# Idle TensorE products in float32r, fourteen of them moved behind the first unit's sums, and the first weight tile's shift done in one piece

## The chip, the cores and the metric

The kernel runs on one core of a Trainium2 chip. A core has TensorE (matrix products; the profile shows its weight loads apart, as PEld), VectorE (DVE), ScalarE (ACT), GpSimd (POOL) and SyncE (SP, which issues the transfers), and 16 DMA engines. The metric is device microseconds of one execution, and the number to compare is the median over runs.

## What is computed

Windowed attention for 4 batches of 576 tokens and 8 heads, then a gated layer, then a soft mixture of 8 experts with 4 slots each. Cut to its core:

```python
attn = softmax(mask(q @ k.T / 8)) @ v        # heads 0-3: window 32; heads 4-7: window 128, every 4th
x = attn as (2304, 512)
x = (sigmoid(x @ w_gate) * (x @ w_val)) @ w_out          # d_ff 1536
logits = x @ phi                                         # 32 slots
h = relu(softmax(logits, axis=tokens).T @ x @ w1) @ w2   # per expert
out = softmax(logits, axis=slots) @ h
```

The three weights of the gated layer come as float64 and are turned into float32 on the chip.

## The kernel before

**Tiling.** Tokens go in five blocks n: four of 512 and a last one of 256. Attention of a block is four units, each a pair of heads. A unit's steps are `scores` (64 small products into two PSUM banks after two mask products, L150 and L164), `soft_max`, `soft_exp`, `soft_sum`, `soft_norm`, `turn_unit` (four transposes on TensorE, L213, and a copy to `pt_ring` on ACT, L214), `sums` (products with the values, L240) and `finish_unit` (the result of each half split into a high part by ACT, L268, and a low part by DVE, L269). The trace shows a float32 product as two weight loads and two products, so the 32 products of `sums` stand there as 64 and 64.

**The gated layer.** For each of 12 column tiles f, 24 products 128x512 in float32r (L488): high and low parts of weights and of tokens. Its weights go through `convert_top` (ACT, L374), `convert_low` (DVE, L381), `convert_shift` (DVE, L378) and `convert_sum` (POOL, L385), and then `split_half` (ACT L445, DVE or POOL L446) into `whl`.

**The start of the program.** `first_block` (L890 to L977) writes out by hand, in program order for each engine, the attention of block 0, the conversion of weight tiles 0 and 1 and the first column tile's products. The order of TensorE there: idle products; scores of units 0 to 2 with idle products between; the transposes of unit 0; idle products; scores of unit 3; the transposes of unit 1; the sums of unit 0; the transposes of unit 2; the sums of unit 1; the first six products of the gated layer; the transposes of unit 3; the sums of unit 2; six products; the sums of unit 3 and 16 tiny ones (`pad_stream`); the last twelve products. The idle products (`keep_warm`, L108) multiply a block of zeros and their result is never read. They keep TensorE occupied between real work. After `first_block`, attention of later blocks is spread between the products of the gated layer, and everything on an engine waits its turn in that engine's queue.

**Names.** `pm` holds the zeros before. `fw` is the tile that is being converted and `st` the raw weights. `x_hi` and `x_lo` are the split tokens, `sm` a unit's softmax weights, `HALVES` and `WHOLE` the two halves or all of a tile's 1024 columns. `WARM` counts the idle products at the very start.

Of the kernel before, what the change touches and what calls it, by code (L numbers as in the profile page):

```python
# [8 lines left out]
F32R = mybir.dt.float32r  # L9
U32 = mybir.dt.uint32  # L10
I32 = mybir.dt.int32
BF16 = mybir.dt.bfloat16
# [5 lines left out]
P = 128  # L18
# [5 lines left out]
HIP = 200  # L24
LA = 2
WO_AT = (12, 13, 14, 15, 16, 17)
WARM = 3
PAD = 8
GA = 0
NRM = True  # L30
ND = 4
# [21 lines left out]
def tile_kernel(  # L53
# [25 lines left out]
    def b8(tag, shape, dt, name):  # L79
        return big.tile(shape, dt, tag=tag, name=name, bufs=BUFS[tag])  # L80
# [16 lines left out]
    pt_ring = b8("bd", [P, 4, 4, 4, 32], F32, "pt_ring")  # L97

    pm = cpool.tile([P, 2, 512], F32, name="pm")
    zero = pm[:, 0].bitcast(BF16)  # L100
    nc.vector.memset(zero, 0.0)
    idle = ps_l1.tile([P, 512], F32, tag="l1", name="idle")

    busy = {}
# [2 lines left out]

    def keep_warm(count):  # L108
        for _ in range(count):
            kept(nc.tensor.matmul(idle, lhsT=zero[:, 0:P], rhs=zero[:, 512:1024], start=True, stop=True))  # L110

    keep_warm(WARM)

# [75 lines left out]
    def soft_exp(u):  # L189
        kp(nc.scalar.activation(u["s"], u["s"], AF.Exp, scale=0.125))  # L190
# [185 lines left out]
    def convert_shift(fw, c):  # L376
        top = fw[:, 0, c].bitcast(U32)
        return kp(nc.vector.tensor_scalar(top, top, 3, None, ALU.logical_shift_left))  # L378

    def convert_low(z, fw, c):  # L380
        kp(nc.vector.tensor_scalar(fw[:, 1, c].bitcast(I32), staged[z][:, c, 0], 2.0**-29, None, ALU.mult))  # L381

    def convert_sum(fw, c):
        top, low = (fw[:, r, c].bitcast(I32) for r in range(2))
        kp(nc.gpsimd.tensor_tensor(low, top, low, ALU.add))  # L385
# [62 lines left out]
    def new_w():  # L448
        return b8("w", [P, 2, 2, ND, P], F32R, "whl")
# [435 lines left out]
    def sums(u, beside=None):  # L885
        if beside is None:
            beside = {"bank": [ps_a.tile([P, 512], F32, tag="a", name=f"x_ps{y}") for y in range(2)]}
        weighted(u, range(2), beside)

    def first_block():  # L890
        u = [{"id": (0, hp), "z": z} for z, hp in enumerate(HP_ORDER)]
        start_unit(u[0], "qk")
        ld(nc.sync.dma_start(msk, masks.bitcast(BF16)))
        start_unit(u[1], "qk")
        start_unit(u[2], "gb")
        ld(nc.sync.dma_start(cst, consts))
        stage(0)
        start_unit(u[3], "gb")
        for z in range(4):
            start_values(u, z)  # L900
        fw = [None, None]
        fw[0] = convert_begin(0)
        scores(u[0], range(4))
        soft_max(u[0])
        soft_exp(u[0])
        keep_warm(1)
        scores(u[1], range(4))
        soft_max(u[1])
        soft_exp(u[1])
        keep_warm(2)  # L910
        soft_sum(u[0])
        soft_norm(u[0], nc.gpsimd)
        scores(u[2], range(4))
        soft_max(u[2])
        soft_exp(u[2])
        soft_sum(u[1])
        soft_norm(u[1], nc.gpsimd)
        keep_warm(4)
        convert_top(0, fw[0], HALVES[0])
        turn_unit(u[0])  # L920
        convert_top(0, fw[0], HALVES[1])
        soft_sum(u[2])
        convert_low(0, fw[0], HALVES[0])
        convert_shift(fw[0], HALVES[0])
        convert_sum(fw[0], HALVES[0])
        soft_norm(u[2], nc.vector)
        convert_low(0, fw[0], HALVES[1])
        convert_shift(fw[0], HALVES[1])
        convert_sum(fw[0], HALVES[1])
        keep_warm(5)  # L930
        scores(u[3], range(4))
        turn_unit(u[1])
        soft_max(u[3])
        sums(u[0], u[2])
        finish_unit(u[0])
        soft_exp(u[3])
        whl = new_w()
        split_half(whl, fw[0][:, 1], 0, nc.vector)
        turn_unit(u[2])
        soft_sum(u[3])  # L940
        soft_norm(u[3], nc.vector)
        split_half(whl, fw[0][:, 1], 1, nc.vector)
        sums(u[1], u[3])
        finish_unit(u[1])
        convert_end(0, fw[0])
        first_qk()
        fw[1] = convert_begin(1)
        first_v()
        g = l1_tile(0, 0)
        pt = [ps_l1.tile([P, 512], F32, tag="l1", name="l1ps") for _ in range(2)]  # L950

        def chunk(dc):
            for a in range(2):
                l1_chunk(0, whl, a, pt[a], dc)

        chunk(HP_ORDER[0])
        turn_unit(u[3])
        for c in HALVES:
            convert_top(1, fw[1], c)
            convert_low(1, fw[1], c)  # L960
            convert_shift(fw[1], c)
            convert_sum(fw[1], c)
        sums(u[2])
        finish_unit(u[2])
        chunk(HP_ORDER[1])
        sums(u[3])
        pad_stream(u[3])
        finish_unit(u[3])
        chunk(HP_ORDER[2])
        whl1 = new_w()  # L970
        for h in range(2):
            split_half(whl1, fw[1][:, 1], h, nc.vector)
        convert_end(1, fw[1])
        chunk(HP_ORDER[3])
        for a in range(2):
            l1_gate(g, a, pt[a])
        return whl1  # L977
# [505 lines left out]
```

## Time and profile before

| | us |
|---|---|
| median of 3 runs | 484.9 (481.81, 484.9, 485.26) |
| the profiled execution, its own time | 486.59 |
| span of the profiled execution, first to last instruction | 484.8 |

| engine | busy us | share of the span |
|---|---|---|
| TensorE products | 466.3 | 96% |
| TensorE weight loads | 359.3 | 74% |
| DVE | 302.9 | 62% |
| ACT | 211.0 | 44% |
| POOL | 157.1 | 32% |

TensorE is the busy engine, and its busy share alone says little on how fast it goes: its clock has two levels, 1.2 and 2.4 GHz, and the profile gives the granted level for any stretch (1.00 is 2.4 GHz, 0.50 is 1.2 GHz). Over the whole span the mean is 0.983. A release named "issue" in the profile means that an engine waited for nothing that the profile records.

### The profile page before, as it was taken

How to read it: one execution, taken by the hardware profiler on the slowest of the kernel's cores; microseconds unless marked ns; L12 is line 12 of the kernel's file. 1: busy time of each engine (PE TensorE's matmuls, PEld its weight loads, DVE VectorE, ACT ScalarE, POOL GpSimd, SP SyncE). 2: the span in 40 equal slices, each digit the busy share in tenths (PEclk: the TensorE clock that was granted, in tenths of full speed). 3: DMA queues.
4: the chain of work that ended last, by engine and by line, in shares of the span. 5: the costliest groups of instructions: out<-in, count | busy, mean ns of one | idle time of the engine just before them, and what ended most of it. 6: DMA issues, size and time to landing. Idle time of an engine off the chain costs nothing.

```text
span 484.8 us, 12657 instructions
## 1 busy us (share of the span) xinstructions
PE 466.3 (96%) x5425; PEld 359.3 (74%) x5425; DVE 302.9 (62%) x595; ACT 211.0 (44%) x397; POOL 157.1 (32%) x134
## 2 busy tenths in 40 slices
PE   7799999999999999999999999999999999999993
PEld 3577788788778778787778888888888889842552
DVE  4868878847768766467876556656547765532623
ACT  2544555534546554454345554554525334300222
POOL 0325555504744654612033342324312124210100
PEclk9869999999999999999999999999999999999997
DMA  8978899786998783222220220201499886689976
GB/s 322 413 279 292 321 336 342 290 283 203 345 354 304 256 315 120 79 89 87 89 87 1 88 78 9 87 19 69 157 372 425 349 327 238 227 293 389 425 254 239
DMA packets 23720, 112.12 MB, mean 231 GB/s; under 512 B 2288, under 2 KB 7152, under 8 KB 14576
## 3 DMA queue, kind: packets, MB, share of 16 engines
q1 hardware_dynamic: 23664, 111.32, 61.7%
q8 instruction: 42, 0.69, 0.6%
q14 instruction: 14, 0.11, 0.1%
HBM read 97.16 MB, written 14.16 MB: 230 GB/s over the span
## 4 chain that ended last, share of the span: by engine, by line
PE 86%; DVE 4%; issue 3%; POOL 2%; ACT 2%; DMA 1%; SPq 0%; POOLq 0%; DVEq 0%; ACTq 0%
PE l1ps L488 30%; PE pa L612 13%; PE pe L612 7%; PE tp L745 4%; PE s_ps L240 3%; PE so_ps L1312 3%; PE pd L612 3%; PE h_ps L1250 3%; PE s_ps L164 3%; PE sp L770 2%; PE lt_ps L716 2%; PE tr L213 2%; POOL fw L385 1%; PE wt_ps L422 1%; PE op L1350 1%
## 5 line engine op out<-in xcount | busy, mean ns | idle before, releaser
L488 PE MATMUL l1ps<-x_hi,whl 128*128 128x512 f32 x384 | 131.4, 407 | 0.8 <-DVE whl L446 0.5
L488 PEld LDWEIGHTS l1ps<-x_hi,whl 128*128 128x128 f32 x384 | 73.1, 190 | 17.7 <-DVE whl L446 1.2
L488 PE MATMUL l1ps<-x_lo,whl 128*128 128x512 f32 x192 | 76.0, 396 | 0.0
L385 POOL TENSOR_TENSOR fw<-fw 128x512 int32<-128x512 int32 x36 | 47.4, 1332 | 51.2 <-DVE fw L378 31.4
L488 PEld LDWEIGHTS l1ps<-x_lo,whl 128*128 128x128 f32 x192 | 36.8, 191 | 6.5
L474 DVE SCALAR_TENSOR_TENSOR g<-g,l1ps 128x512 f32<-128x512 f32 (+1 forms) x36 | 21.4, 595 | 29.2 <-PE l1ps L488 29.2
L488 PE MATMUL l1ps<-x,whl 128*128 128x256 f32 x288 | 37.0, 285 | 0.0
L488 PEld LDWEIGHTS l1ps<-x,whl 128*128 128x128 f32 x288 | 35.4, 192 | 0.4 <-issue 0.2
L499 ACT ACTIVATE g<-l1ps 128x512 f32<-128x512 f32 (+1 forms) x36 | 19.0, 526 | 33.9 <-PE l1ps L488 33.9
L446 POOL TENSOR_TENSOR whl<-w,whl 128x512 fp32r<-128x512 f32 x12 | 15.9, 1327 | 51.2 <-ACT whl L445 39.7
L201 POOL TENSOR_TENSOR sm<-sm,su 128x512 f32<-128x512 f32 x14 | 18.1, 1292 | 27.1 <-DVE su L197 19.4
L745 PEld LDWEIGHTS tp<-cst,g 128*128 128x128 f32 x192 | 21.3, 140 | 5.4 <-issue 4.2
L745 PE MATMUL tp<-cst,g 128*128 128x128 f32 x192 | 25.0, 275 | 0.0
L446 DVE TENSOR_TENSOR whl<-fw,whl 128x512 fp32r<-128x512 f32 x24 | 20.9, 882 | 6.0 <-ACT whl L445 5.3
L750 ACT COPY gt<-tp 128x512 f32<-128x512 f32 x24 | 14.1, 586 | 24.2 <-PE tp L745 21.7
L446 POOL TENSOR_TENSOR whl<-wst,whl 128x512 fp32r<-128x512 f32 x12 | 15.9, 1321 | 25.9 <-ACT whl L445 20.9
L675 DVE TENSOR_TENSOR tm<-pe,tm 128x512 f32<-128x512 f32 x12 | 8.3, 692 | 24.7 <-PE pe L612 24.7
L445 ACT CAST whl<-fw 128x512 fp32r<-128x512 f32 x24 | 14.7, 620 | 19.7 <-POOL fw L385 13.0
L374 ACT ACTIVATE fw<-st 128x1024 f32<-128x1024 f32 (+1 forms) x20 | 21.0, 1057 | 4.5 <-DMA st<-wd 4.5
L240 PE MATMUL s_ps<-pt_ring,v 64*64 64x32 f32 (+1 forms) x992 | 18.3, 220 | 4.1 <-issue 4.0
L445 ACT CAST whl<-wst 128x512 fp32r<-128x512 f32 x24 | 14.3, 618 | 14.2 <-PE l1ps L488 8.6
L446 DVE TENSOR_TENSOR whl<-wst,whl 128x512 fp32r<-128x512 f32 x12 | 14.4, 1197 | 9.5 <-ACT whl L445 9.5
(483 smaller groups left out, 962.6 us busy)
## 6 DMA issues: line engine op xcount, KB each, us to landing
ew<-w SPq DMA_DIRECT2D x32, 1024.0 KB, 7.9
st<-wd SPq DMA_DIRECT2D x18, 1024.0 KB, 7.9
wst<-wg SPq DMA_DIRECT2D x12, 1024.0 KB, 5.9
v<-qkv SPq DMA_DIRECT2D x20, 512.0 KB, 7.2
wg<-fw SPq DMA_DIRECT2D x12, 512.0 KB, 5.6
w<-wg SPq DMA_DIRECT2D x6, 1024.0 KB, 6.4
qk<-qkv SPq DMA_DIRECT2D x10, 576.0 KB, 6.1
qk<-qkv SPq DMA_DIRECT2D x8, 528.0 KB, 6.1
```

What stands on the lines that cost most here:

```text
L164: nc.tensor.matmul(u["s_ps"][r][32 * i : 32 * i + 32, t, :], lhsT=q[64 * r : 64 * r + 64, 128 * t + 32 * i : 128 * t + 32 * i + 32], rhs=k ...
L201: kp(norm.tensor_tensor(s, s, u["su"].unsqueeze(2).to_broadcast([P, 8, 64]), ALU.mult))
L240: nc.tensor.matmul(o, lhsT=v[k, t, i, r, :], rhs=p_[k, 2 * r + t, i, 0:nq], start=True, stop=True)
L374: return kp(nc.scalar.activation(fw[:, 0, c], staged[z][:, c, 1].bitcast(F32), AF.Prelu, scale=2.0**-112, alpha=2.0**32))
L385: kp(nc.gpsimd.tensor_tensor(low, top, low, ALU.add))
L445: kp(nc.scalar.copy(whl[:, 0, h], src[:, h]))
L446: kp(eng.tensor_tensor(whl[:, 1, h], src[:, h], whl[:, 0, h].bitcast(F32), ALU.subtract))
L474: return nc.vector.scalar_tensor_tensor(g, g, 1.0, val, ALU.add, ALU.mult)
L488: nc.tensor.matmul(pt, lhsT=whl[:, w_, a, dc, :], rhs=x_[n][:, dc, :], start=(dc == HP_ORDER[0] and (w_, x_) == (0, x_hi)), stop=(dc == HP ...
L499: return nc.scalar.activation(g, pt, AF.Tanh, scale=0.5) if a == 0 else gated(g, pt)
L612: nc.tensor.matmul(pt, lhsT=w[:, w_, P * c : P * c + P], rhs=x_[:, c], start=first and c == 0 and w_ == 0 and x_ is hi, stop=c == 1 and w_ ...
L745: nc.tensor.transpose(tp[:, c], g_sb[self.n, 4 * q + c][:, P * j : P * j + P], ident)
```

## The change

The idle products are made of float32r operands in place of bfloat16. Their zeros are a 128x128 block in a buffer of the pool `w` (L94 and the following lines of the changed kernel), written by a shorter fill and a copy, and the moving operand reads that block four times. The first group has 8 products in place of 3. The five ahead of unit 3's scores are gone, and a group of 14 (`HOLD`) stands behind the sums of unit 0. On DVE, the first tile's `convert_low` and `convert_shift` are one instruction each over 1024 columns, behind the norm of unit 2; before they were two each over 512 columns, on both sides of that norm. `whl` is allocated one line earlier. All line numbers from there on are larger by 3.

```diff
-WARM = 3
+WARM = 8
+HOLD = 14
@@
-    zero = pm[:, 0].bitcast(BF16)
-    nc.vector.memset(zero, 0.0)
+    nc.vector.memset(pm[:, 0, 0:P], 0.0)
+    zero = b8("w", [P, 2, 2, ND, P], F32R, "zero")[:, 0, 0, 0]
+    nc.vector.tensor_copy(zero, pm[:, 0, 0:P])
+    zeros = zero.unsqueeze(1).to_broadcast([P, 4, P])
@@
-            kept(nc.tensor.matmul(idle, lhsT=zero[:, 0:P], rhs=zero[:, 512:1024], start=True, stop=True))
+            kept(nc.tensor.matmul(idle.rearrange('p (a b) -> p a b', a=4), lhsT=zero, rhs=zeros, start=True, stop=True))
@@ first_block
         soft_sum(u[2])
-        convert_low(0, fw[0], HALVES[0])
-        convert_shift(fw[0], HALVES[0])
-        convert_sum(fw[0], HALVES[0])
         soft_norm(u[2], nc.vector)
-        convert_low(0, fw[0], HALVES[1])
-        convert_shift(fw[0], HALVES[1])
-        convert_sum(fw[0], HALVES[1])
-        keep_warm(5)
+        convert_low(0, fw[0], WHOLE)
+        convert_shift(fw[0], WHOLE)
+        for c in HALVES:
+            convert_sum(fw[0], c)
         scores(u[3], range(4))
         turn_unit(u[1])
         soft_max(u[3])
         sums(u[0], u[2])
+        keep_warm(HOLD)
         finish_unit(u[0])
+        whl = new_w()
         soft_exp(u[3])
-        whl = new_w()
```

TensorE, at the end of unit 0's sums in `first_block`. `s_ps_211` and `s_ps_212` are the two PSUM banks that the sums write, and `tr` the transposes of unit 2. Before:

```order
L240 MATMUL s_ps_211<-pt_ring,v_110 64x32
L240 MATMUL s_ps_212<-pt_ring,v_110 64x32
L213 MATMUL tr<-cst,sm_97 128x128 [waits DVE_49,PE_49]
L213 MATMUL tr<-cst,sm_97 128x128 x3
L240 MATMUL s_ps_286<-pt_ring,v_110 64x32 [waits DMAHW0_49,DVE_49,Activation_49]
```

The same place on TensorE after the change (the banks are now numbered 218 and 219):

```order
L243 MATMUL s_ps_218<-pt_ring,v_117 64x32
L243 MATMUL s_ps_219<-pt_ring,v_117 64x32
L113 MATMUL idle<-zero 128x512 x14
L216 MATMUL tr<-cst,sm_104 128x128 [waits DVE_49,PE_49]
L216 MATMUL tr<-cst,sm_104 128x128 x3
```

Fourteen idle products, which wait for nothing, now stand between the last product of unit 0's sums and the transposes of unit 2.

DVE, from the reciprocal of unit 2 to the softmax of unit 3. Before:

```order
L197 RECIPROCAL su<-su 128x8 [waits DVE_49]
L381 TENSOR_SCALAR fw<-st 128x512 [waits DMAHW5_49]
L378 TENSOR_SCALAR fw<-fw 128x512 [waits Activation_49]
L201 TENSOR_TENSOR sm_97<-sm_97,su 128x512 [waits DVE_49]
L381 TENSOR_SCALAR fw<-st 128x512
L178 TENSOR_REDUCE mx<-s_ps_286 128x4 [waits PE_49]
```

The same place on DVE after the change:

```order
L200 RECIPROCAL su<-su 128x8 [waits DVE_49]
L204 TENSOR_TENSOR sm_104<-sm_104,su 128x512 [waits DVE_49]
L384 TENSOR_SCALAR fw<-st 128x1024 [waits DMAHW5_49]
L381 TENSOR_SCALAR fw<-fw 128x1024 [waits Activation_49]
L181 TENSOR_REDUCE mx<-s_ps_286 128x4 [waits PE_49]
```

The norm of unit 2 moved ahead of the conversion of tile 0, whose four instructions became two.

## Rows read from the trace of the kernel before

**Rows 1.** The page: span, engines' busy us (share) xinstructions, and the instruction queue.
```profile
span 484.8 us, 12657 instructions
...
PE 466.3 (96%) x5425; PEld 359.3 (74%) x5425; DVE 302.9 (62%) x595; ACT 211.0 (44%) x397; POOL 157.1 (32%) x134
...
q8 instruction: 42, 0.69, 0.6%
```

**Rows 2.** Windows: stretch, us, busy (count) of PE, PEld, DVE, ACT, POOL; PEclk, DMA.
```profile
21.00:22.00 1.00, 1.00 (x50) 0.96 (x43) 0.47 (x1) 1.00 (x3) 0.00 (x0) 0.80 1.09 453
...
31.00:32.00 1.00, 1.00 (x47) 1.00 (x48) 0.00 (x0) 0.00 (x0) 0.05 (x1) 0.58 0.98 410
```

**Rows 3.** Timeline of PE in the first block: start, us, instructions [idle before <-releaser].
```profile
5.07 0.61 PE L150 MATMUL s_ps<-msk 128*128 128x256 bf16 x2 [2.15 <-DMA msk<-masks]
...
13.08 1.24 PE L110 MATMUL idle<-pm 128*128 128x512 bf16 x5
...
15.85 1.13 PE L240 MATMUL s_ps<-pt_ring,v 64*64 64x32 f32 x63
19.86 0.19 PE L240 MATMUL s_ps<-pt_ring,v 64*64 64x32 f32 x1 [2.88 <-issue]
19.99 0.65 PE L213 MATMUL tr<-cst,sm 128*128 128x128 f32 x4
20.57 1.13 PE L240 MATMUL s_ps<-pt_ring,v 64*64 64x32 f32 x64
...
29.10 1.05 PE L488 MATMUL l1ps<-x_hi,whl 128*128 128x512 f32 x2
29.95 0.63 PE L488 MATMUL l1ps<-x_lo,whl 128*128 128x512 f32 x1
...
33.20 0.63 PE L488 MATMUL l1ps<-x_hi,whl 128*128 128x512 f32 x2
33.67 0.39 PE L488 MATMUL l1ps<-x_lo,whl 128*128 128x512 f32 x1
...
35.51 0.39 PE L150 MATMUL s_ps<-msk 128*128 128x256 bf16 x2
```

**Rows 4.** Windows again, for the counts of TensorE's products and weight loads.
```profile
0.00:18.00 18.00, 13.13 (x350) 7.51 (x351) 10.85 (x27) 5.77 (x9) 3.93 (x7) 1.00 0.91 354
19.80:143.50 123.70, 122.51 (x1911) 98.12 (x1910) 89.89 (x169) 62.12 (x109) 55.92 (x43) 0.96 0.86 306
137.17:143.50 6.33, 5.97 (x129) 4.75 (x127) 5.65 (x12) 4.63 (x10) 5.00 (x4) 1.00 1.00 353
```

**Rows 5.** Timeline of PE, sums of a later block.
```profile
144.21 0.55 PE L240 MATMUL s_ps<-pt_ring,v 64*64 64x32 f32 x24 [1.07 <-issue]
```

**Rows 6.** Timeline of DVE: unit 2's norm, a half tile, and later a whole tile.
```profile
15.85 0.69 DVE L201 TENSOR_TENSOR sm<-sm,su 128x512 f32<-128x512 f32 x1
16.45 1.49 DVE L381 TENSOR_SCALAR fw<-st 128x512 int32<-128x512 uint32 x1
...
34.92 0.69 DVE L381 TENSOR_SCALAR fw<-st 128x1024 int32<-128x1024 uint32 x1
```

**Rows 7.** Timelines of POOL and ACT around the gap.
```profile
16.01 1.64 POOL L385 TENSOR_TENSOR fw<-fw 128x512 int32<-128x512 int32 x1 [0.97 <-DVE fw L378]
...
17.04 0.37 ACT L268 CAST x_hi<-s_ps 128x256 fp32r<-128x256 f32 x1 [0.49 <-PE s_ps L240]
20.09 0.37 ACT L268 CAST x_hi<-s_ps 128x256 fp32r<-128x256 f32 x1 [2.68 <-PE s_ps L240]
```

**Rows 8.** Timeline of PE from 132 to 138 us.
```profile
132.51 0.86 PE L164 MATMUL s_ps<-qk 64*32 64x64 f32 x64
...
134.36 0.66 PE L422 MATMUL wt_ps<-cst,fw 128*128 128x128 f32 x4
...
137.18 0.39 PE L488 MATMUL l1ps<-x_lo,whl 128*128 128x512 f32 x1
```

**Rows 9.** Windows: the end of the program.
```profile
478.00:480.00 2.00, 0.00 (x0) 0.00 (x0) 0.25 (x1) 0.00 (x0) 0.00 (x0) 0.75 1.03 342
```

## The prediction

> **What bounds the kernel now.** I read the page first, then TensorE's timeline of the first 36 us, then its clock by windows, then DVE, ACT and POOL around the place that changes. TensorE is busy 96% of 484.8 us [rows 1], so a microsecond taken from its path is a microsecond of time, unless another engine is late in its place. The change touches only the start, up to the first mask product of the next block at 35.51 [rows 3].
>
> Two things cost time there. First, TensorE stands still for 2.88 us before the last of the 64 products of unit 0's sums, which starts at 19.86 [rows 3]. ACT takes the first half of the sums at 17.04 and waits 2.68 us for the second [rows 7], and its queue (unit 3's exponentials, the weight split) stands behind that wait. Second, the clock: the mean of the slice 21 to 22 is 0.80 and of 31 to 32 is 0.58 [rows 2]; with levels 1.0 and 0.5 that is a fall at 21.6 and a rise at 31.84, so 10.2 us at 1.2 GHz. What that costs is seen in float32r products: pairs start 0.85 us apart at 29.10 and 0.47 at 33.20 [rows 3], 0.425 and 0.235 for one.
>
> **Why TensorE stands still at 16.98.** The releaser is "issue": the profile knows of nothing waited for. The product held back is the last of a group whose 63 others ran, and its weights are loaded (350 products, 351 loads so far) [rows 4]. So this is no wait for data. Count instructions: 701 ran before the gap [rows 4]. A second such gap, 1.07 us, stands in the middle of other sums at 144.21 [rows 5], and between the two there are 1911 + 1910 = 3821 [rows 4]. The page's instruction queue made 42 transfers, 0.69 MB, for 10850 products and loads [rows 1]: 16.4 kB and 258 of them in each. 3821 is 14.8 times 258, and from 137.17 to the second gap there are exactly 129 + 127 = 256 [rows 4]. With 256 to a block, and a few semaphore instructions that the counts leave out, both gaps open where a new block of instructions begins. I take them as waits for the next block of TensorE's own program, whose transfer competes with data: the DMA share is 0.91 up to 18 us and 1.00 before the second gap [rows 4].
>
> In the Trainium skill, "Runtime: NRT & Kernel Launch", "Instruction fetch mechanics", instructions come in 16 KiB blocks of 256, one fetched while another runs, and the crossing is "mostly hidden". The trace agrees on the blocks and not on the hiding: 2.88 and 1.07 us stand open. Were it hidden here, the gap would have another cause, and the sum would be that of rival A.
>
> **The change, part by part.**
>
> *Eight products at the start.* Five more, 5 x 0.425 = 2.1 us, inside the 2.15 us that TensorE waits for the masks anyway [rows 3]: nothing. Without that cover they would cost 2.1.
>
> *Five products fewer ahead of unit 3's scores.* They take 1.24 us [rows 3]. The scores can start up to 1.24 earlier (not at all if their keys land later), and the sums reach the block's edge up to 1.24 earlier. The edge stays where it is in the program: before it 3+1+2+4+5 = 15 idle products stood, now 8+1+2+4 = 15, each a load and a product. So the same product waits for the same block, which comes when DMA delivers it. I leave that at 19.86; the gap only gets longer, 2.9 to 4.1 us.
>
> *DVE.* One instruction of 0.69 replaces the second half's 1.49, which ran while POOL was adding from 16.01 to 17.65 [rows 6, 7]. DVE gets some 1.2 us earlier to unit 3's softmax. POOL starts its sums later by about as much. Both end before 20.09, when ACT gets the second half of the sums and the chain goes on [rows 7]. Nothing; if the block came early, up to 1.2 gained.
>
> *Fourteen products.* They stand behind the held product, so in the next block, and cannot start before 19.9. They cost 14 x 0.235 = 3.3 us at the upper level and 14 x 0.425 = 6.0 at the lower; nothing only if they ran in the gap. Behind them in TensorE's queue stand unit 2's transposes, for which ACT's copy and then its cast of the second weight half wait, unit 1's sums, and all products of the layer.
>
> *From there to the end of the first block*, at the upper level: the transposes of units 2 and 3, 2 x 0.65; three sums at some 1.07 (1.13 less overlap); 24 products x 0.235 = 5.6; the tiny ones 0.15: 10.2 us. Before, from 19.99 to 35.51, it was 15.5 [rows 3]. If the 14 products end at X, the block ends at X + 10.2.
>
> *The clock.* It fell 1.6 us after a gap of 2.88 with sums around it, and at the very end it falls within the slice 478 to 480, with TensorE idle [rows 9]. The gap now is longer, so I expect it to fall again, in the gap or just behind it. It rose again at 31.84 after float32r products and sums without a pause since 28.1. The 14 products are such an unbroken stretch, so I expect the rise some 3.8 us into them, at about 23.7: nine products by then, five more x 0.235, X = 24.9. The block ends at 35.1, a gain of **0.4 us**. Bounds: no fall, X = 23.2, gain 2.1; lower level through all 14 and on, rival C.
>
> *Later block edges.* The program is longer by 14 products and 14 loads, so each later block begins 28 instructions earlier in the work. The gap at 144.21 falls away, as the edge moves out of the sums: **-1.07**. But the block that begins at 137.18 [rows 8] will begin 28 instructions earlier, at the work of 134.36. That block was there at 137.18, but nothing says that it was there 2.8 us earlier: its fetch can only start once the block before is entered, in the scores at about 132.6, and the block after it took from 137.18 to 144.21, 7.0 us. Bounds 0 and 2.8; the 7.0 us row is nearest and speaks for late; I take **+2.4**.
>
> **Sum.** -0.4 - 1.07 + 2.4 = +0.9 us. On the profiled execution's own 486.59 that is 487.5; that execution was 1.7 over the median of 484.9. On the median: **485.8**.
>
> **Rivals.**
>
> A. *The products fill the gap.* If the gap is not a missing block, the 14 products run from 15.7 to 17.0 on, 3.3 us, to 19.0 to 20.3, the clock stays up, and the block ends at 29.2 to 30.5: a gain of 5.0 to 6.3, no block terms, 479.3. For it: 14 products are just longer than the gap. Against it: the releaser, the loaded weights, the counts.
>
> B. *The products come late, and the clock does not fall.* X = 23.2, gain 2.1; with the block terms +1.3: 484.1. For it: the products are dense right behind the gap. Against it: the longer gap.
>
> C. *The lower level lasts.* If it again lasts 10.2 us, from about 18.2 to 28.4, the 14 products take 6.0 (to 25.9), the transposes and sums behind them some 2.5 to 28.4, and what is left, 10.2 - 0.65 - 1.07 = 8.5, ends at 36.9: 1.4 lost; with the block terms 487.6. It decides as soon as the rise comes later than 25. For it: the one low stretch seen is that long.
>
> D. *The block at 137 is in time.* Then -0.4 - 1.07: 483.4.
>
> **How the numbers follow.** Forecast 0.45, with a range of its own of 484 to 488; A 0.08, B 0.17, C 0.15, D 0.15. Runs of the same kernel lie 3.5 us apart, which I add by halves to both sides. 8 in 10: leave out A and the edge of C: 481.5 to 488.8. About 1% (4.85 us) is what a measurement of this kernel can tell from no change. Faster by over 1% needs A: 0.08. Slower by over 1% needs C with the new gap in full and the spread on top: 0.05. Within: 0.87.
>
> **What would show it.** In the profile after: 63 products of unit 0's sums, then a gap of over 2.9 us released by "issue", the last product at about 19.9, and the 14 idle products behind it, not in it. The granted clock falls before 21 and rises between 22.6 and 26. The first mask product of the next block at about 35.1. No gap in the sums at 144, and a new one released by "issue" at about 134. I am wrong if the idle products start at 16 to 17, if the gap has gone, or if the clock stays up from 12 us on.

## The result and the profile after

The kernel after takes 487.0 us (median of 16 runs, 485.15 to 491.1) where the kernel before takes 483.85 (16 runs on the same chip): a ratio of 1.0067, 95% interval 1.0047 to 1.0088, that is 2.3 to 4.3 us more. Every ratio in this document is taken against runs of the kernel before on the same chip, made together with the kernel in question. It is within 1%, as forecast; the forecast of 485.8 lay 0.9 above the median then known for the kernel before, and the measured difference is 3.2.

The profiled execution has a span of 485.5 us (own time 487.29) and a mean granted clock of 0.990, against 484.8, 486.59 and 0.983 before. TensorE's timeline of its start (start, us, instructions, idle time before and its releaser), to be held beside [rows 3]:

```profile
1.31 3.51 PE L113 MATMUL idle<-zero 128*128 128x512 f32 x8 [1.31 <-DVE zero L103]
...
13.38 0.86 PE L167 MATMUL s_ps<-qk 64*32 64x64 f32 x64 [1.20 <-DMA qk<-qkv]
...
14.75 1.13 PE L243 MATMUL s_ps<-pt_ring,v 64*64 64x32 f32 x63
18.54 0.21 PE L243 MATMUL s_ps<-pt_ring,v 64*64 64x32 f32 x1 [2.66 <-issue]
18.68 6.32 PE L113 MATMUL idle<-zero 128*128 128x512 f32 x14
24.82 0.62 PE L216 MATMUL tr<-cst,sm 128*128 128x128 f32 x4
...
35.28 0.39 PE L153 MATMUL s_ps<-msk 128*128 128x256 bf16 x2
```

The gap is still there, in front of the same 64th product, and the 14 idle products stand behind it. They take 6.3 us and end at 24.8. Its windows (columns as in [rows 2]) show the clock falling just after 18 and rising shortly before 25; the third row counts instructions from the fourth unit's scores to the gap:

```profile
18.00:19.00 1.00, 0.46 (x2) 0.32 (x2) 0.00 (x0) 0.21 (x1) 0.31 (x1) 0.51 0.97 407
24.00:25.00 1.00, 1.00 (x5) 0.70 (x4) 0.00 (x0) 0.00 (x0) 0.00 (x0) 0.57 0.97 365
...
13.37:18.00 4.63, 2.50 (x131) 2.14 (x132) 3.97 (x10) 1.18 (x3) 2.35 (x3) 1.00 1.04 426
18.50:135.80 117.30, 115.12 (x1783) 92.99 (x1783) 83.32 (x156) 57.25 (x100) 51.04 (x39) 0.97 0.86 307
```

The last row runs up to the other new thing, a gap in the later work; the sums at 144, which were cut in [rows 5], now run through:

```profile
135.85 0.60 PE L425 MATMUL wt_ps<-cst,fw 128*128 128x128 f32 x4 [2.19 <-issue]
...
143.81 1.14 PE L243 MATMUL s_ps<-pt_ring,v 64*64 64x32 f32 x64
```

From the held product to this gap there are 1783 + 1783 = 3566 products and loads, where [rows 4] had 3821 between the two gaps: 255 fewer, one block of 256 (with a semaphore instruction or two that the counts leave out). The gap is at the weight transposes that stood at 134.36 in [rows 8], where the forecast put it.

ACT waits for the held product 2.48 us, and then, for the first time, 5.28 us for the transposes that stand behind the 14 products. [rows 7] had the first of these waits, of 2.68:

```profile
18.79 0.37 ACT L271 CAST x_hi<-s_ps 128x256 fp32r<-128x256 f32 x1 [2.48 <-PE s_ps L243]
...
25.48 0.59 ACT L217 COPY pt_ring<-tr 128x512 f32<-128x512 f32 x1 [5.28 <-PE tr L216]
```

Compared profile to profile, the first block ends 0.23 us earlier (35.28 for 35.51) and the new gap is 1.12 longer than the one that went: these two executions differ by only 0.7 us. The medians differ by 3.2. The experiments had to find where the rest is.

### The profile page after: what moved, and what is told of

Same layout as the page of the kernel before. It is cut to its first block, busy times and chain, and to the rows that moved or that the text cites. A ratio compares the mean times of both kernels' runs of the same rounds, so it can differ in the third digit from the quotient of the medians.

```text
span 485.5 us, 12683 instructions
## 1 busy us (share of the span) xinstructions
PE 466.7 (96%) x5438; PEld 362.4 (75%) x5439; DVE 301.5 (62%) x594; ACT 211.5 (44%) x397; POOL 156.8 (32%) x134
## 4 chain that ended last, share of the span: by engine, by line
PE 87%; DMA 5%; DVE 2%; issue 1%; ACT 1%; POOL 1%; SPq 1%; DVEq 0%; ACTq 0%; POOLq 0%
PE l1ps L491 31%; PE pa L615 13%; PE pe L615 7%; PE tp L748 4%; PE s_ps L243 3%; PE so_ps L1313 3%; PE pd L615 3%; PE h_ps L1251 3%; PE s_ps L167 3%; DMA w<-wg 3%; PE sp L773 2%; PE lt_ps L719 2%; DMA qk<-qkv 2%; PE tr L216 2%; PE wt_ps L425 1%
## 5 line engine op out<-in xcount | busy, mean ns | idle before, releaser
L491 PE MATMUL l1ps<-x_hi,whl 128*128 128x512 f32 x384 | 129.0, 401 | 0.0
L491 PEld LDWEIGHTS l1ps<-x_hi,whl 128*128 128x128 f32 x384 | 72.1, 188 | 15.5 <-issue 0.4
L449 POOL TENSOR_TENSOR whl<-wst,whl 128x512 fp32r<-128x512 f32 x12 | 15.9, 1322 | 25.9 <-ACT whl L448 20.9
L448 ACT CAST whl<-fw 128x512 fp32r<-128x512 f32 x24 | 14.7, 620 | 19.4 <-POOL fw L388 13.4
```

What stands on the lines that cost most here:

```text
L448: kp(nc.scalar.copy(whl[:, 0, h], src[:, h]))
L449: kp(eng.tensor_tensor(whl[:, 1, h], src[:, h], whl[:, 0, h].bitcast(F32), ALU.subtract))
L491: nc.tensor.matmul(pt, lhsT=whl[:, w_, a, dc, :], rhs=x_[n][:, dc, :], start=(dc == HP_ORDER[0] and (w_, x_) == (0, x_hi)), stop=(dc == HP ...
```

## The experiments

A word on names: "edges" are the places in TensorE's program at which a new block of 256 instructions begins. An idle product is two instructions (a load and a product), a tiny one of `pad_stream` four.

### Moving only the edges

In the kernel after, the later edges put back where they were:

```diff
-PAD = 8
+PAD = 1
```

> The kernel after the change with 7 of its 8 tiny float32 products taken out (28 instructions fewer, all behind the first block), so that everything later in TensorE's program stands where it stood in the kernel before; the 14 idle products stay. My theory (the edges of later blocks of TensorE's program): the gap of 2.19 us at 135.9 goes, the one of about 1.1 us in the sums at 144 comes back, and the time is about 1.1 us under the kernel after (some 486). If the whole difference between the medians (3.2 us) came from moved edges, it is back at the kernel before, 484. Rival (the 14 products cost it, in the first 36 us): no change against the kernel after, 487, less 0.15 us for the tiny products, with the first block's end as in the kernel after.

Measured: 484.32 us, ratio 0.9986 (0.9963 to 1.0009). The kernel after stood at 1.0067, so 28 tiny instructions fewer are worth some 3.9 us, where I had expected 1.1, or 3 if all of the difference lay in the edges. The gap at 135 is gone, and one stands again in the sums of [rows 5]; the 14 products are where they were. The clock was low for only 3.4 us behind the first gap (19.2 to 22.6), where the kernel after, whose program is the same up to 31 us, had 6.8. The gap in TensorE's timeline, and two windows (columns as in [rows 2]):

```profile
142.34 0.55 PE L243 MATMUL s_ps<-pt_ring,v 64*64 64x32 f32 x24 [0.77 <-issue]
...
19.00:20.00 1.00, 0.93 (x3) 0.72 (x3) 0.31 (x1) 0.71 (x2) 0.00 (x0) 0.60 0.98 402
22.00:23.00 1.00, 1.00 (x5) 0.83 (x4) 0.90 (x4) 0.00 (x0) 0.00 (x0) 0.69 1.05 401
```

In the kernel before, only the later edges moved:

```diff
-PAD = 8
+PAD = 15
```

> The kernel before with 7 more tiny float32 products (28 instructions more, behind the first block), so that the later edges stand as in the kernel after the change, and nothing else. Theory of the edges: the gap at 144 goes, one of about 2.2 us opens at about 136, and the time is 1.1 us over the kernel before, with some 0.15 us more for the tiny products; up to 3 us over if all of the difference lies in the edges. Rival (the idle products alone): the time of the kernel before within 0.3 us. First 36 us as in the kernel before under both.

Measured: 486.17 us, ratio 1.0045 (1.0022 to 1.0068): 1.1 to 3.3 us slower, without any idle product added. The rival, no change within 0.3 us, is out. TensorE's timeline and its windows show why a gap of 2.46 costs more than 2.46:

```profile
134.40 0.60 PE L422 MATMUL wt_ps<-cst,fw 128*128 128x128 f32 x4 [2.46 <-issue]
...
136.35 1.05 PE L488 MATMUL l1ps<-x_hi,whl 128*128 128x512 f32 x2
...
140.52 0.62 PE L488 MATMUL l1ps<-x_hi,whl 128*128 128x512 f32 x2
```

and its windows (columns as in [rows 2]):

```profile
134.00:136.00 2.00, 1.60 (x9) 1.36 (x9) 1.38 (x3) 1.64 (x2) 0.00 (x0) 0.90 1.02 292
136.00:138.00 2.00, 2.00 (x6) 1.58 (x5) 1.66 (x6) 0.96 (x2) 1.91 (x2) 0.50 1.04 348
138.00:140.00 2.00, 2.00 (x13) 1.65 (x11) 1.30 (x3) 0.48 (x1) 0.60 (x1) 0.75 0.95 360
```

The mean clock is 0.90, 0.50 and 0.75 in three stretches of 2 us, so it fell at 135.6 and rose at 139.0: 3.4 us at 1.2 GHz, in which a pair of products takes 1.05 us in place of 0.62, and a price of 1.7 us on top of the gap. The first profile of the kernel after has a gap of 2.19 there and a clock of 1.00 behind it, so such a gap brings the clock down in some executions and not in others.

### Both kernels once more

> The kernel before as it is, once more, for another profiled execution. My theory of what was mis-sized: the execution profiled first had an unusually long stretch at the lower clock (10.2 us, first block's end at 35.5), where the kernel before with only its later edges moved, whose first 36 us are the same program, showed 6.5 us and 33.0. Then this one shows a low stretch of 6 to 7 us and the first block's end at 32.5 to 33.5. Rival: 10 us and 35.5 are its usual state and the other was the odd one. Time 484 to 485 in both.

Measured: 484.2 us, ratio 1.0010 (0.9991 to 1.0029), span 482.1. The start of this execution, TensorE's timeline and the clock:

```profile
14.67 0.86 PE L164 MATMUL s_ps<-qk 64*32 64x64 f32 x64
...
20.27 0.21 PE L240 MATMUL s_ps<-pt_ring,v 64*64 64x32 f32 x1 [3.10 <-issue]
...
33.40 0.39 PE L150 MATMUL s_ps<-msk 128*128 128x256 bf16 x2
```

and its windows (columns as in [rows 2]):

```profile
19.00:20.00 1.00, 0.00 (x0) 0.00 (x0) 0.94 (x3) 0.00 (x0) 0.63 (x1) 0.57 0.91 379
25.00:26.00 1.00, 1.00 (x3) 0.65 (x3) 1.00 (x4) 0.00 (x0) 0.00 (x0) 0.51 1.05 418
```

It fell at 19.1 and rose at 26.0: 6.8 us at the lower level, not the 10.2 of [rows 2], and the block ends at 33.40, not 35.51 [rows 3], although the held product starts 0.4 later here. Of the three profiles of this start (this one, the first, and the one with only the later edges moved, which has 6.8 and 32.99) the one on which the forecast was built is the only one with 10.2.

> The kernel after as it is, once more, beside its variants on one chip. Summed from single steps (moved edges +2.2, start of 8 products with the norm's order about -1 to -2, 14 products +1.5 to 2 with the edges as before or as after): 486.5 to 488. Where the clock falls at the new gap near 135, as it did in the kernel before with moved edges, the stretch 134 to 140 has a mean clock under 0.8; where it doesn't, it is 1.00, as in the first profile.

Measured: 487.48 us (7 runs), ratio 1.0077 (1.0047 to 1.0108). The difference repeats. Here the held product starts at 19.78, 6.2 us after the fourth unit's scores began, behind a gap of 3.23; the first profile had 18.54 and 2.66. This time the clock does fall behind the new gap, by its windows from 137.4 to 140.8:

```profile
13.58 0.93 PE L167 MATMUL s_ps<-qk 64*32 64x64 f32 x64 [0.18 <-DMA qk<-qkv]
...
19.78 0.21 PE L243 MATMUL s_ps<-pt_ring,v 64*64 64x32 f32 x1 [3.23 <-issue]
...
136.18 0.60 PE L425 MATMUL wt_ps<-cst,fw 128*128 128x128 f32 x4 [1.91 <-issue]
```

and its windows (columns as in [rows 2]):

```profile
136.00:138.00 2.00, 1.82 (x9) 1.59 (x9) 1.49 (x3) 1.64 (x2) 0.02 (x1) 0.85 0.90 276
138.00:140.00 2.00, 2.00 (x6) 1.52 (x5) 1.56 (x6) 0.96 (x2) 2.00 (x2) 0.50 1.00 366
140.00:142.00 2.00, 2.00 (x13) 1.71 (x12) 1.49 (x4) 0.71 (x2) 0.51 (x2) 0.80 0.99 383
```

Its first block ends at 35.90.

### The 14 products taken out

From the kernel after, with its later edges kept:

```diff
-HOLD = 14
-PAD = 8
+HOLD = 0
+PAD = 15
```

> The kernel after without its 14 idle products behind the sums, with 7 tiny products more in their place later, so that the later edges stand as in the kernel after. What differs from the kernel after is the price of the 14 products alone. My theory: without them the clock stays low to about 31, the first block ends 0.2 to 0.5 us later than in the kernel after (35.5 to 35.8), and the time is the same within 0.5 us or up to 0.5 us slower, 487 to 487.5. Rival (the products are a net cost of some 2 us in most executions): 2 us faster than the kernel after, 485. Rival (the products do gain as meant, clock up for ten us): 2 us slower, 489.

Measured: 484.43 us, ratio 0.9999 (0.9978 to 1.0020): some 3.3 us under the kernel after. The gap at the weight transposes is still there, 1.82 us at 133.52, without a fall of the clock in this execution. The first block ends at 32.52, 2.8 earlier than in the kernel after, not later. The products are a net cost here, as the first of the two rivals said; my own theory, no change or up to 0.5 us slower, was wrong.

The same with the edges of the kernel before (`HOLD = 0`, `PAD = 8`), so that only the start of the change is left:

> The kernel after without the 14 products, 8 tiny ones as in the kernel before, so that every later edge stands as in the kernel before: what is left of the change is its 8 products at the start, the 5 fewer ahead of the fourth unit's scores, and the scaling over the whole tile. My theory: the scores start some 0.7 us earlier, so does everything behind them, also the arrival of the held block (18.8 against 19.2 to 19.9), first block's end 32.4 to 32.6; time 0.5 to 2 us under the kernel before, 482.8 to 484.3. Rival (the block comes when DMA delivers it, whatever is crossed when): last product of the sums at 19.9 as before, no change, 484.8.

Measured: 483.43 us, ratio 0.9992 (0.9974 to 1.0010): the rest of the change is worth nothing that can be told from zero. The held product starts at 18.83, where I had expected 18.8, 5.2 us after the scores of the fourth unit began at 13.62; by the rival it would have come at 19.9 as before. The low stretch of this execution was again one of 10.2 us (20.8 to 31.0) and its block ends at 34.56, which the expectation did not allow for.

```profile
18.83 0.19 PE L243 MATMUL s_ps<-pt_ring,v 64*64 64x32 f32 x1 [2.63 <-issue]
```

The part on DVE alone, in the kernel before:

```diff
-        convert_low(0, fw[0], HALVES[0])
-        convert_shift(fw[0], HALVES[0])
-        convert_sum(fw[0], HALVES[0])
...
-        convert_low(0, fw[0], HALVES[1])
-        convert_shift(fw[0], HALVES[1])
-        convert_sum(fw[0], HALVES[1])
+        convert_low(0, fw[0], WHOLE)
+        convert_shift(fw[0], WHOLE)
+        for c in HALVES:
+            convert_sum(fw[0], c)
         keep_warm(5)
```

> The kernel before with one part of the change alone: the first tile's scaling and shift over the whole tile in one instruction each, behind the third unit's norm; all idle products as before. My prediction's step: VectorE and GpSimd are hidden here, nothing, 484 within 1 us. Rival: the norm of the third unit comes earlier or the weight split later, and the first block's end moves by over 0.5 us against 33.0 to 33.4.

Measured: 484.38 us, ratio 0.9999 (0.9979 to 1.0018). The block ends at 32.51, where the other profiles of this start with a low stretch of 6.8 us have 32.99 and 33.40: 0.5 to 0.9 us earlier, one execution against another, and nothing in the time.

### Is it the edge that opens the gap, and when does its block come

Idle products in the gap, by having them ahead of the edge: none at the start, 8 behind the sums.

```diff
-WARM = 8
-HOLD = 14
+WARM = 0
+HOLD = 8
```

> The kernel after with no idle products at the start and 8 behind the first unit's sums in place of 14: 15 in all up to there, as stood ahead of the sums before, so that all of the sums and nearly all of the 8 products lie in the block of TensorE's program that was loaded already, and the later edges stand as in the kernel before. My theory (the wait belongs to the edge): the 64 products of the sums run without a gap, ACT's second shifted half starts near 16, the idle products run at once behind them, and a gap released by issue stands at or behind the last of them, up to about 19.9; the first block ends 1 to 5 us earlier than in the kernel after, time 482 to 485. Rival (the wait belongs to the last product of the sums, whatever stands ahead): 63 products, a gap, and the idle products behind it, as in the kernel after; time 485 to 487.

Measured: 483.93 us, ratio 0.9992 (0.9970 to 1.0014). TensorE's timeline:

```profile
14.45 0.86 PE L167 MATMUL s_ps<-qk 64*32 64x64 f32 x64 [0.97 <-DMA qk<-qkv]
...
15.83 1.14 PE L243 MATMUL s_ps<-pt_ring,v 64*64 64x32 f32 x64
16.89 1.89 PE L113 MATMUL idle<-zero 128*128 128x512 f32 x7
20.64 0.42 PE L113 MATMUL idle<-zero 128*128 128x512 f32 x1 [1.86 <-issue]
```

All 64 products run, ACT gets both halves at once, and the gap has moved behind seven idle products: the wait belongs to the place in the program and not to the sums. But the block comes 6.2 us after the scores began, at 20.64, the clock falls at 20.9 all the same, and the block ends at 34.36.

The first three edges 16 instructions earlier in the work, without the 14 products:

```diff
+    for _ in range(10):
+        kept(nc.tensor.matmul(idle[:, 0:64], lhsT=zero, rhs=zero[:, 0:64], start=True, stop=True))
     keep_warm(WARM)
...
-WARM = 8
-HOLD = 14
-PAD = 8
+WARM = 6
+HOLD = 0
+PAD = 4
```

> As the kernel after without the 14 products, but with 10 narrow idle products (64 columns) in place of two of the 8 wide ones at the start, inside the wait for the masks, and 4 tiny ones fewer later: the first three edges stand 16 instructions earlier in the work, the later ones as in the kernel before. My theory: a block is there about 5.1 us after TensorE crossed the edge before it (13.40 to 18.54 in the kernel after, 13.91 to 19.07, 14.37 to 19.21, 13.68 to 18.76 in the variants). The edge before the gap then no longer lies in the fourth unit's scores, which wait for their keys to 13.6, but ahead of the first transposes, crossed at 11.7 to 12.3: the block is there at 16.8 to 17.4, and the gap, now 8 products before the end of the sums, is 1.0 to 1.6 instead of 2.6; time 1 to 2 us under the same kernel with the edges where they were, and up to 5 if the clock then stays up. Rival (the block comes when DMA delivers it): the gap stays and ends at 18.8 or later, time unchanged.

Measured: 484.11 us, ratio 1.0002 (0.9983 to 1.0022). The ten narrow products took 0.22 us each, more than I had allowed for, so all the work began 1.2 late, which spoils the comparison of times. My theory's figures failed: the gap was to shrink to 1.0 to 1.6 and end by 17.4, and it is 2.85 and ends at 19.77, with the time unchanged, as the rival said. What neither had reckoned with is that the edge before it would stand open too. That the gaps belong to the edges is clearest here:

```profile
12.86 0.44 PE L218 MATMUL tr<-cst,sm 128*128 128x128 f32 x2 [0.91 <-POOL sm L206]
13.95 0.44 PE L218 MATMUL tr<-cst,sm 128*128 128x128 f32 x2 [0.66 <-issue]
...
15.91 1.01 PE L245 MATMUL s_ps<-pt_ring,v 64*64 64x32 f32 x55
19.77 0.32 PE L245 MATMUL s_ps<-pt_ring,v 64*64 64x32 f32 x9 [2.85 <-issue]
```

and its windows (columns as in [rows 2]):

```profile
13.94:18.00 4.06, 2.97 (x127) 2.38 (x128) 3.96 (x9) 1.93 (x4) 1.66 (x2) 1.00 1.04 426
```

Between the two there are 127 + 128 = 255 instructions: one block, and 5.8 us from the one edge to the other, of which TensorE had work for 3. The edge that used to lie in the fourth unit's scores has been moved to the first transposes and opens a gap of its own there. As that edge was crossed only at 13.95, the 19.77 fits both the theory (5.8 us behind it) and the rival, and this kernel does not tell them apart.

### Filling the gap further

Fifteen idle products in all, 3 at the start, 2 ahead of the first transposes and 10 behind the sums; and all 15 behind the sums:

```diff
-WARM = 8
-HOLD = 14
+WARM = 3
+HOLD = 10
...
-        keep_warm(1)
...
-        keep_warm(2)
...
-        keep_warm(4)
+        keep_warm(2)
```

> The kernel after with 15 idle products in all, as many as stood ahead of the held product before, but spread so that 3 stand at the start, 2 ahead of the first transposes and 10 behind the first unit's sums (none between the first three units' scores): all 15 lie in the block that is loaded, and later edges stand as in the kernel before. Theory (the gap lasts until some 5.2 us after the edge before it, which lies in the fourth unit's scores, is crossed; products that lie ahead of the next edge fill it for nothing): the 64 products of the sums run through, the 10 idle ones take 2.4 us behind them, and a gap of at most 1 us stands at their end, at 18.5 to 20. If such a gap is too short for the clock to fall, the first block ends at 30 to 31.5 (10.2 us at the upper level behind it) and the time is 2 to 3 us under the kernel before, 481 to 482. Rival (the clock falls all the same, or does not get up in time with so few products ahead): end at 33 to 35, time 484 to 486.

> The same with all 15 idle products behind the first unit's sums and none ahead. Theory: 15 x 0.235 = 3.5 us of products, from about 16 to 19.6 at the upper level, no gap or one under 0.5 us, then as above with the block some 0.5 us later: first block's end 30.5 to 32, time 481.5 to 483. Rival (products ahead are needed for the clock at 12 to 16): scores and sums at the lower level, 1.18 and 1.93 us for 64 products in place of 0.86 and 1.13, which makes it 1 to 3 us later: 484 to 487.

Measured: 483.31 us, ratio 0.9990 (0.9971 to 1.0009), and 483.96, 0.9992 (0.9969 to 1.0015). With ten, the gap is down to 1.40 and the clock stays up through it. It falls later, at 21.8, and the next edge, which nothing waited at before, now opens:

```profile
19.86 0.39 PE L113 MATMUL idle<-zero 128*128 128x512 f32 x1 [1.40 <-issue]
...
27.22 0.43 PE L243 MATMUL x_ps<-pt_ring,v 64*64 64x32 f32 x16 [1.03 <-issue]
...
33.36 0.39 PE L153 MATMUL s_ps<-msk 128*128 128x256 bf16 x2
```

So the block ends at 33.36, as without the products and as the rival said, and not at the 30 to 31.5 of the theory. With all fifteen behind the sums there is no gap at all, but TensorE goes at its lower pace up to the idle products, as the rival said:

```profile
14.38 1.18 PE L167 MATMUL s_ps<-qk 64*32 64x64 f32 x64
...
18.41 5.43 PE L113 MATMUL idle<-zero 128*128 128x512 f32 x15
...
34.13 0.39 PE L153 MATMUL s_ps<-msk 128*128 128x256 bf16 x2
```

### A whole block more

> The kernel after with 57 tiny float32 products more in place of the 7 fewer of the first experiment: 57 x 4 = 228 instructions, which with the 28 of the change make 256, one whole block, so that every later edge again stands at the work at which it stood in the kernel before. Theory of the edges: the gap near 135 to 137 goes, the one in the sums at 143 to 145 comes back at 0.4 to 1.1 us, the mean granted clock over the runs is near 0.991 as in the first experiment and not 0.987 as in the kernel after; the tiny products cost 57 x 0.017 = 1.0 us (30 records take 0.43 us in place of 16 in 0.31), so the time is some 484.2 + 1.0 = 485.2, under the kernel after in spite of more work. Rival (it was the number of tiny products, or the 14 idle ones as such): 487.3 to 488.5, the kernel after plus 1.0.

Measured: 489.09 us (6 runs), ratio 1.0092 (1.0055 to 1.0128): 0.6 above even the rival's 487.3 to 488.5, and the mean granted clock is 0.989, not 0.991. The edges did as the theory says: no gap at the weight transposes, and one of 0.23 in the sums at 145.82. What the profile shows of the loss is in the first block and just behind it, where new gaps stand:

```profile
33.72 1.04 PE L878 MATMUL pad<-pt_ring,v 128*32 128x8 f32 x103 [0.49 <-issue]
...
37.54 0.39 PE L153 MATMUL s_ps<-msk 128*128 128x256 bf16 x2
...
43.37 0.30 PE L167 MATMUL s_ps<-qk 64*32 64x64 f32 x3 [0.39 <-issue]
```

From the pad's start at 32.81 to its end at 34.76 it is 1.9 us, in place of 0.2 in the first experiment. That is 1.7, and 0.39 at 43.37. The low stretch was 6.8 us in this execution, for 3.4 in the first experiment, and put the pad 1.4 later. By the landmarks of the next section, the first block ends 3.0 later than in the first experiment, 0.95 more is lost up to the next landmark, and nothing behind it: across the edge region it takes 19.51, as the kernels with old edges do. So this kernel's loss does not lie at the later edges. But its profile is of an execution of 487.69, and for the 1.4 by which the median is higher there is no profile; that stays open.

### Where the difference sits

The same three landmarks can be read from every timeline: the mask products of the second block's first unit (the end of the first block), those at 132.19 in the kernel before, just ahead of the scores in [rows 8], and the second such group behind them (152.56). Between them:

| kernel | idle products | later edges | low stretch behind the first gap | end of first block | to the next landmark | across the edge region | from there to the last group of products |
|---|---|---|---|---|---|---|---|
| before, first profile | old | old | 10.2 | 35.51 | 96.68 | 20.37 | 322.80 |
| before, second profile | old | old | 6.8 | 33.40 | 96.68 | 19.75 | 322.83 |
| before, norm alone | old | old | 6.8 | 32.51 | 96.72 | 19.08 | 324.21 |
| after without the 14, old edges | 8 | old | 10.2 | 34.56 | 96.72 | 19.77 | 323.24 |
| after, `PAD` 1 | 8, 14 | old | 3.4 | 34.51 | 96.14 | 20.05 | 322.44 |
| before, `PAD` 15 | old | moved | 6.8 | 32.99 | 96.70 | 23.14 | 324.16 |
| after without the 14, moved edges | 8 | moved | 6.8 | 32.52 | 96.67 | 21.10 | 322.46 |
| after, first profile | 8, 14 | moved | 6.8 | 35.28 | 96.14 | 21.29 | 323.38 |
| after, second profile | 8, 14 | moved | 6.8 | 35.90 | 96.12 | 22.56 | 324.23 |

The last column varies by 1.8, and most of that is the clock once more. The three kernels with 324.2 are those whose clock is low for another 3.4 us between 424 and 435, with old edges (the norm alone) and with moved ones; 24 products there take 4.43 us in place of 2.78. Less the 1.7 that such a stretch costs, the means for moved and old edges are 322.7 and 322.8. The norm alone, its window (columns as in [rows 2]), and the same products in the first profile of the kernel before:

```profile
424.68 4.43 PE L1224 MATMUL si_ps<-wos,fin 128*32 128x512 f32 x24
...
426.00:428.00 2.00, 2.00 (x12) 0.38 (x8) 0.00 (x0) 0.00 (x0) 0.00 (x0) 0.50 0.37 45
...
429.19 2.78 PE L1226 MATMUL si_ps<-wos,fin 128*32 128x512 f32 x24
```

Two others carry the difference. Across the edge region the four profiles with moved edges take 22.0 us on the mean, the five others 19.8: 2.2. The five profiles that are not in the table, all with old edges, take 19.4 to 20.3, so moved and old do not overlap. The first block ends at 35.2 on the mean of the three with the 14 products and at 33.6 on the mean of the six without: 1.6, of which 0.55 come back up to the next landmark (96.13 for 96.70). Together 2.2 + 1.6 - 0.55 = 3.3, beside 3.2 measured. The 1.6 hangs on which low stretches these nine executions happened to have: where it is 6.8, the two with the products end at 35.6 and the four without at 32.9, 2.7 apart. How often each length comes is not known, so that the sum falls so near is in part luck.

What this account leaves open: by it, the 14 products alone should cost about 1 us and the moved edges alone about 2. With the edges moved, the products cost 3.3 (1.0067 against 0.9999); with the old edges, nothing (0.9986 against 0.9992). The moved edges cost 3.9 with the products (1.0067 against 0.9986), 2.2 in the kernel before and, without the products, 0.3 in the kernel after (0.9999 against 0.9992). Each of these has an uncertainty of 1 to 1.5 us, and the difference between 3.9 and 0.3 one of about 2. So noise alone does not cover it: taking out either part gave back the whole loss, and that the two prices are simply added is not shown.

The mean granted clock over all runs of a kernel does not settle it. With the 14 products it is 0.987 with moved edges and 0.991 with old ones, without them 0.986 with both: the products go with a higher clock where the edges are old, which is the direction of the times. But the kernel before has 0.987 to 0.988, no more than the kernel after, at 3 us less. And the mean takes in the end of the program, where TensorE has no work and the clock is low for 2.6 to 5.8 us in the profiles, a spread nearly as large as the difference in question (0.004 in a mean over 485 us is a stretch of 3.9 us at half speed). That a low stretch at 136 comes in most executions of the kernel after is not shown either; it was seen in one of two profiles.

## Why the prediction was right, and where it was off

**The bound and the gap.** Right. The gap is still ahead of the 64th product, released by "issue", with the 14 products behind it; the fall of the clock before 21 and the rise between 22.6 and 26 came at 18.0 and 24.9. Rival A is out, since nothing ran in the gap; rival B, since the clock fell; rival C, which needed a rise later than 25, though only just, since it came at 24.9 and in the second profile at 24.7; rival D, since the new gap came. That the wait belongs to the edge, which was inferred from counts, is shown by the kernel with eight products behind the sums and by the one with ten narrow products, in which the gap moved with the program. Two of the counts were weaker than they read: nothing says that all 42 transfers of instructions were TensorE's, and the 256 from 137.17 were counted back from the gap, as nothing opens at 137.17. The 255 between two open edges need neither.

**The arrival of the held block.** Wrong in one profile and right in the other, and it changed little. I left it at 19.86 and expected a longer gap, 2.9 to 4.1; the first profile had 2.66, at 18.54, the second 3.23, at 19.78. The edge before it lies among the first ten instructions of the fourth unit's scores (263 instructions from 13.37 to the gap), and in the twelve profiles in which it lies at the start of those scores and the block was waited for, the block was there 4.9 to 6.2 us after they began: 14.67 to 20.27 in the second profile of the kernel before, 13.38 to 18.54 and 13.58 to 19.78 after, 13.62 to 18.83 without the products. The arrivals themselves lie between 18.5 and 20.6. A delay that spreads by 1.3 us fits better than a time of its own that spreads by 2.1, but the kernel meant to tell the two apart did not, so this rule is likely and not shown. The prediction had used it for the edge at 137 (its fetch can only start once the block before is entered) and not for this one. In the Trainium skill, "Runtime: NRT & Kernel Launch", "Instruction fetch mechanics", a block is fetched while the one before it runs; the 5.8 us between the two open edges are in keeping with that. Its "mostly hidden" does not hold here, as the first profile already showed.

**The term that was mis-sized: the clock, -0.4.** The end of the products, 24.9, and of the block, 35.1, came out near (24.8 and 35.28 by the first profile, 25.5 and 35.90 by the second). From the one to the other it took 10.5 and 10.4, where the prediction has 10.2 (its pieces add up to 10.3). In the first profile the end of the products came out by two misses that cancel. They began 1.2 earlier than assumed (18.7 for 19.9), and the rise, forecast 3.8 us into them at 23.7, came at 24.9, so that all 14 ran at the lower level. With `PAD` 1 it came 3.4 us into them, and in the second profile 4.8. The 3.8 had been counted from 28.1, but in the kernel before TensorE had been without a pause since 24.64, as its timeline shows:

```profile
24.64 0.79 PE L488 MATMUL l1ps<-x_hi,whl 128*128 128x512 f32 x1 [0.51 <-DVE whl L446]
```

What was wrong in size is what the ends were held against. 35.51 is the end in an execution whose low stretch lasted 10.2 us; three others of the same start, or of it with the norm moved, had one of 6.8 and ended at 32.5 to 33.4. If the 14 products shorten a low stretch of 10.2, one of 6.8 passes in 6.8 with them as well (18.0 to 24.9), so that they are added work at the lower level. Against 33.6, the mean of the six profiles without them, the term is +1.6, or +1.1 with the 0.55 that come back. The range took in the spread of whole runs but not that of the term; that 487.0 lies in it is owed to that width and not to the sizes of the terms.

**The later edges, -1.07 and +2.4.** The place was right to the instruction and the gap nearly so: 2.19 and 1.91 in the two profiles of the kernel after, 2.46 and 1.82 in those with moved edges alone. What comes back is less than 1.07: of the other nine profiles with old edges, eight have 0.17 to 1.02 there and one has nothing. What was missed is that a gap of this size can take the clock with it: 1.7 us more in two of these four profiles. The prediction priced this at the first gap and not at the second.

**Start and DVE at nothing.** Right: the start and the norm together measure -0.4 (0.9992), the norm alone 0.0 (0.9999), both within their uncertainty.

**No kernel beats both.** Ratios of 0.9986 to 0.9992 are the best, and none of their intervals is clear of 1. A gap that is filled or moved comes back at the next edge, or the pace at the start is lost.

## What to carry to other kernels

Where an engine stands still for "issue" at a place that is a whole number of instruction blocks from another such gap, count instructions before changing anything: a product added in one place moves every later edge, and the cost can fall 100 us further on, where the diff shows nothing. Keep the count constant when work without a result is put in or taken out; a whole block more did keep the later edges in place here, but its 57 products opened new gaps where they stood. And price a term that hangs on the clock from more than one profile: one execution's low stretch was half as long again as the next one's (10.2 and 6.8 us), or twice as long (6.8 and 3.4).

## What the runs showed of the hardware that was not expected

- A block of instructions arrived 4.9 to 6.2 us after the edge before it was crossed, with the DMA share near 1.0, while TensorE had work for 3 us in that block: small products run through 256 instructions faster than the next 256 are delivered.
- The granted clock of the profile does not show the pace at the start. With all fifteen idle products late, the scores at 14.38 took 1.18 us for 64 products (0.86 later on, at 34.45), and the first eight idle products of the kernel after take 0.44 each, as at 1.2 GHz, while the granted clock is given as 1.00. A window of the kernel with all fifteen late (columns as in [rows 2]):

```profile
14.00:16.00 2.00, 2.00 (x70) 1.45 (x68) 1.90 (x4) 1.23 (x3) 1.04 (x1) 1.00 1.02 418
```

- The low stretch that follows the first gap was 3.4 us long in two profiles, 6.8 in most and 10.2 in two, for nearly the same program. The kernel before had both 6.8 and 10.2; the kernel after and the one with `PAD` 1, one program up to 31 us, had 6.8 and 3.4.
